# Delta rule, routed experts and a second FFN on one core: key products made further ahead, fewer conversions beside the last expert, token rows of block 1 fetched later

## The chip, the cores and the metric

One core of a Trainium2 chip runs one program that holds all three parts. The metric is the device time of one execution in microseconds (us). Three runs of the kernel before took 973.56, 974.29 and 976.66 us; the median, 974.29, is the time that the change is compared with.

## The reference

The first part is a delta rule over 768 tokens for 4 x 8 heads of size 48; the second sends each of 3072 tokens to one of 8 experts; the third is an FFN with squared ReLU.

```python
for t in range(S):                       # 768 tokens, state 48 x 48 per head
    y[:, :, t] = einsum('bhd,bhde->bhe', q[t], state)
    v_old = einsum('bhde,bhd->bhe', state, kt)          # kt: normalized key
    state += bt * einsum('bhd,bhe->bhde', kt, vt - v_old)
x = y.reshape(3072, 384)
expert_idx = argmax(xn @ en.T / tau)                    # one expert per token
out[mask] = gate_w * (relu(x[mask] @ w1[e]) @ w2[e])    # 8 experts, 384-1024-384
h = relu(out @ w_in)                                    # 384-2048
result = (h * h) @ w_out                                # 2048-384
```

## The kernel before

**Delta rule (0 to about 271 us).** The 768 tokens are 24 chunks of 32, and each chunk is a step `s` of one loop (`attention`). A step is a chain: the state `Sb` gives `ch` (L313), VectorE (DVE) writes half of `Ub` (L324) and ScalarE (ACT) the other half (L334), TensorE (PE) multiplies by the chunk's inverse table (L343), DVE and ACT copy that to `Wb` (L324, L356), PE adds to the state (dS, L362), ACT copies the state out (L372). A step is marked in the trace by DVE's `Ub` at L324; step 0 starts at 49.28 us.

The inverse tables are made by DVE for four chunks at once, a *stream* (`lanes`, L236 on): 31 rounds of a product (`mul`, L269, into `tmp`) and a sum (`acc`, L277, into `TL`). `acc` of a round reads what its `mul` wrote, and the next `mul` reads what `acc` wrote. `fill(now, part)` issues such operations at fixed places of a step, so many as the pace of the open streams asks for; with two streams open it takes from them by turns.

A stream needs the products of keys with keys of its four chunks. `gram(s)` (L154) makes them for one chunk, on PE, between W (L343) and the state's update (L362); ACT empties the two banks into `GPs` and `Pm` (L174). After every fourth chunk SP, the queue that issues most transfers, writes them to DRAM and reads them back in another layout (L176, L179, L184, L188). `gram(s)` needs the chunk's keys and queries, which `load_kq` fetches, three chunks to a buffer `W`, also on SP. SP, PE, DVE and ACT each work through their own instructions strictly in program order.

**Experts (about 272 to 556 us).** For expert e PE makes the hidden rows block by block (`fb` 0 to 7); ACT and DVE split each into two parts (`hh`, `hl`, L1173, L1174). `ht` (L1184) is their sum for the last 64 slots, which PE reads at L1208. Between these, the 64-bit numbers of `w_in` and `w_out` are turned into 32-bit ones on DVE and ACT, in 28 pieces of six operations each (`w64`, L1070 to L1090), and written to DRAM by a POOL queue transfer (L1083); `run(due, now, nq)` issues `nq` of these operations. Their buffers `t2k` are two, and `ht` and the one-hot tables of the last tokens (`ohs`, L1245) take turns in the same two. `place` (L926) multiplies by those tables; its result are rows of the second FFN's first block.

**Second FFN (about 556 us to the end).** 8 blocks of 384 tokens. `load_x2(n)` (L1135) fetches block n's token rows from DRAM, where the scatters of the experts (L1216) wrote them; `weights` fetches the converted pieces (L602) and splits them (L576, L579) during block 0.

Of the kernel before, what the change touches and what calls it, by code (L numbers as in the profile page):

```python
# [8 lines left out]
F32 = mybir.dt.float32  # L9
# [12 lines left out]
def kernel(  # L22
# [102 lines left out]

    def load_kq(s):
        if s % 3 == 0:
            KQ3[0] = cp.tile([128, 3, 4, 4, 2, C], F32, name="W", bufs=5)
        a = KQ3[0][:, s % 3]
        KQ[s] = a[:, :, :, 0], a[:, :, :, 1], a  # L130
        nc.sync.dma_start(a, kq[s])
# [14 lines left out]
    def gram(s, n0=0, n1=2, banks=GP2):  # L146

        g, i = divmod(s, 4)
        n = n1 - n0
        for p in range(4):  # L150
            for h2 in range(2):
                for b in range(4):
                    r = 64 * h2
                    PE.matmul(  # L154
                        banks[h2][C * b : C * b + C, p * n * C : (p + 1) * n * C],
                        KQ[s][0][r : r + 64, p, b],
                        KQ[s][n0][r : r + 64, p, b]
                        if n == 1
                        else KQ[s][2][r : r + 64, p, b].rearrange("d n j -> d (n j)"),
                        start=True,  # L160
                        stop=True,
                    )
        if i == 0 and n0 == 0:
            GPs[g] = gp.tile([128, 4, 8, C], F32, name="GPs", bufs=3)
        if i == 0 and n1 == 2:
            Pm[g] = gp.tile([128, 4, 4, 2, C], F32, name="Pm", bufs=3)
        for m in range(n0, n1):
            for h2 in range(2):
                if m == 0:
                    o = GPs[g][:, i].rearrange("p (x a c) j -> p c x a j", x=2, c=2)[:, h2]  # L170
                else:
                    o = Pm[g][:, :, i].rearrange("p (a c) x j -> p c x a j", c=2)[:, h2]
                src = banks[h2][:, : 128 * n].rearrange("p (x a n j) -> p n x a j", x=2, a=2, n=n)
                A.activation(o, src[:, m - n0], AF.Copy)  # L174
        if i == 3 and n0 == 0 and g > 1:
            nc.sync.dma_start(gscr[g % 2].rearrange("b i u j -> (b i) (u j)"), GPs[g].rearrange("p s h j -> p (s h j)"))  # L176
            ALs[g] = wp.tile([128, C, C], F32, name="AL", bufs=3)
            for b in range(4):
                nc.sync.dma_start(ALs[g][C * b : C * b + C], gscr[g % 2][b].rearrange("i u j -> u i j"))  # L179
        if i == 3 and n1 == 2:  # L180
            scr = pscr[g % 2]
            PL2[g] = gp.tile([128, 4, 4, 2, C], F32, name="PL2", bufs=4)
            for b in range(4):
                nc.sync.dma_start(  # L184
                    scr[:, :, b, :].rearrange("f j x -> j f x"),
                    Pm[g][C * b : C * b + C].rearrange("p f s c j -> p f (s c j)"),
                )
            nc.sync.dma_start(  # L188
                PL2[g].rearrange("p b s c j -> p (b s c j)"), scr.rearrange("f j b x -> (f j) (b x)")
            )  # L190
# [450 lines left out]
    def attention():  # L641
# [129 lines left out]
        for s in range(NS):  # L771
            g, i = divmod(s, 4)
            last = g == NG - 1
            while s not in ready:
                streams[0].pop()
            if s:
                mmV(s, 0)
                mmV(s, 1)
                mm1K(s, 0)
                mm1K(s, 1)  # L780
            U(s)
            fill(s, 0.25)
            if s:
                mm1Q(s)
            if s > 0:
                xT = xrt(s - 1)
            while streams and streams[0].g <= g:
                streams[0].pop()
            W(s, 0)
            W(s, 1)  # L790
            if s == NS - 1:
                lows.pop(0)()
            if s == 0:
                for b in range(4):
                    masked(0, b)
            if ahead < min(15 if s < 4 else NS, s + 12):
                gram(ahead)
                ahead += 1
            if scats and s >= E:
                drain(route_q)  # L800
                scats.pop(0)()
            fill(s + 0.25, 0.4)
            if s == NS - 4:
                first_x()
            if s >= NS - 3:
                pre1(s - NS + 3, False)
            if scats and s >= NS - 10:
                scats.pop(0)()
            if R is not None and s in (6, 10, 14, 17, 19):
                drain(route_q)  # L810
                R[1]()
                queue(R[2])
                scats += R[3]
            if s > 0:
                xlog(s - 1, xT)
                if i == 0 or s == 18:
                    R = route(g, 0, 2) if i else route(g - 1, 2 if s == 20 else 0, 4)
                    R[0][0]()
                    queue(R[0][1:])
                    if last and i == 0:  # L820
                        drain(route_q)
            if s + 1 < NS:
                dS(s, 0)
                dS(s, 1)
            if s == NS - 1:
                R = route(NG - 1, 2, 3)
                for o in R[0]:
                    o()
            PW(s)
            if last and i == 0:  # L830
                R[1]()
                queue(R[2])
                scats += R[3]
            if s <= E:
                padding(s)
            if i == 3 and g + 2 < NG:
                load_v(g + 2)
                load_k2(g + 2)
            if s % 3 == 2:
                for n in range(s + 13, min(s + 16, NS)):  # L840
                    load_kq(n)
            if ahead % 4 == 0 and ahead // 4 - 1 > made:
                made += 1
                streams.append(Stream(made, s + 1.6))
            fill(s + 0.65, 0.35)
            if s in (15, 17, 20):
                pre1((15, 17, 20).index(s), True)
            if s in (NS - 3, NS - 2):
                R = route(g, s - NS + 3, s - NS + 4)
                for o in R[0] + [R[1]] + R[2]:  # L850
                    o()
                scats += R[3]
# [241 lines left out]
    def moe():  # L1094
# [48 lines left out]
        for e in range(E):  # L1143
# [21 lines left out]
            for fb in range(8):  # L1165
# [11 lines left out]
                if fb == 3 and e + 1 < E:  # L1177
                    load_x(e + 1)
                if e:
                    run(fb + 1, 4, 2 if e + 1 == E else (1, 1, 0, 1, 0, 1, 0, 1)[fb])  # L1180
                else:
                    run(fb + 1, (0, 0, 0, 0, 2, 4, 6, 9)[fb], 1)
            ht = mp.tile([128, 8, 64], F32, name="t2k", bufs=2)
# [66 lines left out]
        for o in late:  # L1250
            o()
        for n in range(NBLK):
            if n + 1 < NBLK:
                load_x2(n + 1)
            xhn, xln = xh[f"a{n}"], xl[f"a{n}"]
            sh, sl = [
# [4 lines left out]
            for fb in range(16):  # L1261
# [13 lines left out]
                def part2(fb=fb, s2=s2, sh=sh, sl=sl):  # L1275
                    A.activation(sh[fb], s2, AF.Copy)
                    V.tensor_tensor(sl[fb], s2, sh[fb].bitcast(F32), ALU.subtract)

                if n == 0:
                    weights(10 * E + 2 + (fb + 1) * 8 // 15)  # L1280
            part2()
# [76 lines left out]
```

## Time and profile before

| | us |
|---|---|
| median of three runs | 974.29 |
| profiled execution | 973.39 |
| its span, first to last instruction | 971.6 |
| PE busy | 908.7 (94%) |
| DVE busy | 620.7 (64%) |
| ACT busy | 443.6 (46%) |
| steps 4 to 15 of the delta rule | 119.75, of which DVE is busy 107.85 |

The profiled execution is 0.9 us below the median, and 1.8 us of it lie around the span. The busy shares are means over three stages. From about 271 us on PE is busy nearly without a gap; in the delta rule its busy time contains stretches at a lower clock and small products that wait for nothing but the chain.

### The profile page before, as it was taken

The numbers are of one execution on the slowest core, as the hardware profiler recorded it, in microseconds if no ns is written. First come the engines' busy times: TensorE is split into PE (matmuls) and PEld (weight loads), VectorE is DVE, ScalarE is ACT, GpSimd is POOL, SyncE is SP. The second block draws the span as 40 slices with busy tenths as digits, with TensorE's granted clock in tenths as the row PEclk, the third lists the DMA queues.
The fourth block names the chain that finished last, engine by engine and source line by source line (L and its number), as shares of the span: only waits on it lengthen the run. The fifth ranks groups of instructions, "written<-read, shape, count | busy, mean of one in ns | idle before, by whom it ended". The sixth has DMA issues, their size and how long they took to land. (4 is left out here: it accounts for less than half of the span.)

```text
span 971.6 us, 22202 instructions
## 1 busy us (share of the span) xinstructions
PE 908.7 (94%) x8982; PEld 810.4 (83%) x8982; DVE 620.7 (64%) x1641; ACT 443.6 (46%) x1051; POOL 89.4 (9%) x126
## 2 busy tenths in 40 slices
PE   4778889899999999999999899999999999999998
PEld 3456667677777798888887689999999999999998
DVE  7999997899667888888789572423334241516060
ACT  2247656557734555455555362423333242415150
POOL 2000012011211122212211200000000000000000
PEclk7579988789989999999999999999999999999999
DMA  8667865441145677477557450101010101010000
GB/s 322 204 186 230 251 172 191 102 144 58 65 142 187 214 245 243 133 245 252 175 181 241 147 163 17 33 9 42 9 41 9 41 9 41 1 49 1 25 1 25
DMA packets 70608, 117.75 MB, mean 121 GB/s; under 512 B 22659, under 2 KB 48746, under 8 KB 70496
## 3 DMA queue, kind: packets, MB, share of 16 engines
q1 hardware_dynamic: 60784, 94.08, 30.4%
q0 software_dynamic: 5440, 15.88, 4.3%
q10 hardware_dynamic: 4272, 6.28, 2.0%
q8 instruction: 72, 1.18, 0.5%
q14 instruction: 40, 0.33, 0.1%
HBM read 84.12 MB, written 32.89 MB: 120 GB/s over the span
## 5 line engine op out<-in xcount | busy, mean ns | idle before, releaser
L1272 DVE TENSOR_TENSOR t4k<-t2k 128x384 f32<-128x384 f32 x128 | 71.4, 558 | 231.9 <-ACT t2k L1271 231.3
L277 DVE TENSOR_TENSOR TL<-TL,tmp 128x31 f32<-128x31 f32 (+15 forms) x186 | 62.7, 340 | 3.6
L269 DVE TENSOR_TENSOR tmp<-AL,TL 128x31 f32<-128x31 f32 (+15 forms) x186 | 62.4, 339 | 3.3
L1121 PE MATMUL gp<-wb,hh 128*128 128x384 f32 x184 | 62.9, 342 | 0.0
L1123 PE MATMUL gp<-wb,hl 128*128 128x384 f32 x184 | 62.0, 337 | 0.6 <-DVE hl L1174 0.6
L1122 PE MATMUL gp<-wb,hh 128*128 128x384 f32 x184 | 61.8, 336 | 0.0
L372 ACT ACTIVATE Sb<-sp 48x384 f32<-48x384 f32 x92 | 44.6, 484 | 34.0 <-PE sp L362 32.5
L1121 PE MATMUL sp<-xh,W 128*128 128x384 f32 (+1 forms) x150 | 51.0, 340 | 2.2 <-ACT t2k L1271 2.2
L1122 PE MATMUL yp<-xl,W 128*128 128x384 f32 (+1 forms) x153 | 52.6, 344 | 0.1
L1121 PE MATMUL yp<-xh,W 128*128 128x384 f32 (+1 forms) x153 | 52.5, 343 | 0.2 <-ACT xh L950 0.2
L1123 PE MATMUL yp<-xh,W 128*128 128x384 f32 (+1 forms) x153 | 52.6, 344 | 0.0
L1123 PE MATMUL gp<-xh,W 128*128 128x384 f32 (+1 forms) x153 | 52.1, 340 | 0.0
L1121 PE MATMUL gp<-xh,W 128*128 128x384 f32 (+1 forms) x153 | 52.0, 340 | 0.0
L1122 PE MATMUL gp<-xl,W 128*128 128x384 f32 (+1 forms) x153 | 51.9, 340 | 0.0
L362 PE MATMUL sp<-Wb,kL 128*48 128x96 f32 x736 | 49.5, 291 | 2.3 <-issue 1.4
L1121 PE MATMUL xp<-wb,hh 128*128 128x384 f32 x152 | 51.3, 338 | 0.0
L1123 PE MATMUL sp<-xh,W 128*128 128x384 f32 (+1 forms) x150 | 51.2, 341 | 0.0
L1123 PE MATMUL xp<-wb,hl 128*128 128x384 f32 x152 | 51.1, 336 | 0.0
L1122 PE MATMUL xp<-wb,hh 128*128 128x384 f32 x152 | 51.1, 336 | 0.0
L1122 PE MATMUL sp<-xl,W 128*128 128x384 f32 (+1 forms) x150 | 50.9, 340 | 0.0
L1216 POOL DMA_INDIRECT x<-y,rows x32 | 35.4, 1105 | 127.2 <-ACT y L1213 72.6
L362 PEld LDWEIGHTS sp<-Wb,kL 128*48 128x48 f32 x736 | 41.7, 149 | 6.0 <-ACT Wb L356 2.6
(314 smaller groups left out, 2463.7 us busy)
## 6 DMA issues: line engine op xcount, KB each, us to landing
W<-in_moe_w_dram SPq DMA_DIRECT2D x42, 256.0 KB, 3.6
W<-in_kq_dram SPq DMA_DIRECT2D x20, 512.0 KB, 7.0
hb<-in_moe_w_dram SPq DMA_DIRECT2D x24, 384.0 KB, 3.3
t4k<-in_moe_w_in_dram SPq DMA_DIRECT2D x12, 512.0 KB, 4.2
t4k<-in_moe_w_out_dram SPq DMA_DIRECT2D x16, 384.0 KB, 3.7
W<-wscr SPq DMA_DIRECT2D x16, 384.0 KB, 4.1
xs<-padrow ACTq DMA_DIRECT2D x8, 693.0 KB, 5.1
xe<-xs SPq DMA_DIRECT2D x8, 594.0 KB, 8.3
```

The source lines that it names most:

```text
L269: V.tensor_tensor(tv[0], AL[:, j, j + 1 :].unsqueeze(1).broadcast_to([128, n, m]), T[:, :n, j : j + 1].broadcast_to([128, n, m]), ALU.mult,)
L277: V.tensor_tensor(T[:, : j + 1, j + 1 :], T[:, : j + 1, j + 1 :], tv[0], ALU.add)
L362: PE.matmul(SP_[hq][64 * par : 64 * par + D, b * 96 : b * 96 + 96], kL2[g][:, i, b * 2 + hq], Wb[hq].rearrange("p b (m r) e -> p b r m e", ...
L372: A.activation(Sb[hq][r : r + D, :, :, par, :], SP_[hq][r : r + D, 0:384].rearrange("p (b m e) -> p b m e", b=4, m=2), AF.Copy,)
L1121: PE.matmul(ps, hs, rh, start=first, stop=False)
L1122: PE.matmul(ps, hs, rl, start=False, stop=False)
L1123: PE.matmul(ps, ls, rh, start=False, stop=last)
L1216: to_x2 = lambda n=n, t=t, y=y, rows_e=rows_e: G.indirect_dma_start(out=x2, out_offset=bass.IndirectOffsetOnAxis(ap=rows_e[:n, t : t + 1]. ...
L1272: V.tensor_tensor(s2, r, r, ALU.mult)
```

## The change

- Delta rule: `gram` may run up to 15 chunks ahead and not 12, and from step 2 on a step may make two chunks' products, until the lead is reached. With that the loads of keys and queries move: chunks 15 to 17 are fetched in step 0 into a buffer of their own, and the later ones three steps earlier. A stream is opened as soon as its four chunks' products are issued. `GPs` and `Pm` have two buffers and not three.
- Last expert: the conversions beside its hidden blocks are 2, 2, 2, 2, 2, 2, 0, 0 operations per block and not 2 in each; the rest stands later.
- Second FFN: the rows of block 1 are asked for in block 0 at `fb` 9, and no longer before block 0.

```diff
     def load_kq(s):
         if s % 3 == 0:
-            KQ3[0] = cp.tile([128, 3, 4, 4, 2, C], F32, name="W", bufs=5)
+            KQ3[0] = (wp if s == 15 else cp).tile([128, 3, 4, 4, 2, C], F32, name="W", bufs=1 if s == 15 else 5)
...
-            GPs[g] = gp.tile([128, 4, 8, C], F32, name="GPs", bufs=3)
+            GPs[g] = gp.tile([128, 4, 8, C], F32, name="GPs", bufs=2)
...
-            Pm[g] = gp.tile([128, 4, 4, 2, C], F32, name="Pm", bufs=3)
+            Pm[g] = gp.tile([128, 4, 4, 2, C], F32, name="Pm", bufs=2)
...
-            if ahead < min(15 if s < 4 else NS, s + 12):
-                gram(ahead)
-                ahead += 1
+            for _ in range(2 if s > 1 else 1):
+                if ahead < min(15 if s < 3 else 18 if s < 4 else NS, s + 15):
+                    gram(ahead)
+                    ahead += 1
...
+            if s == 0:
+                for n in range(15, 18):
+                    load_kq(n)
...
             if s % 3 == 2:
-                for n in range(s + 13, min(s + 16, NS)):
+                for n in range(s + 16, min(s + 19, NS)):
                     load_kq(n)
-            if ahead % 4 == 0 and ahead // 4 - 1 > made:
+            while ahead // 4 - 1 > made:
                 made += 1
                 streams.append(Stream(made, s + 1.6))
...
-                    run(fb + 1, 4, 2 if e + 1 == E else (1, 1, 0, 1, 0, 1, 0, 1)[fb])
+                    run(fb + 1, 4, ((1, 1, 0, 1, 0, 1, 0, 1), (2, 2, 2, 2, 2, 2, 0, 0))[e + 1 == E][fb])
...
         for n in range(NBLK):
-            if n + 1 < NBLK:
+            if 0 < n < NBLK - 1:
                 load_x2(n + 1)
...
+                if n == 0 and fb == 9:
+                    load_x2(1)
```

By this, `gram` runs for chunk 12 in step 0, 13 in step 1, 14 in step 2, 15 and 16 in step 3, 17 and 18 in step 4, and 19 to 23 in steps 5 to 9; before it ran for chunk s + 11 in each of the steps 1 to 12. The streams of chunks 12 to 15, 16 to 19 and 20 to 23 open in steps 3, 5 and 9, and before in 4, 8 and 12.

**DVE in step 7**, right behind `Wb`. Names are the buffers: `AL` the products, `TL` the table, `tmp1` the product of a round; `sm` a small table of a newly opened stream. Before:

```order
L269 TENSOR_TENSOR tmp1_2246<-AL_1714,TL_1949 128x156
L277 TENSOR_TENSOR TL_1949<-TL_1949,tmp1_2246 128x6x26
L269 TENSOR_TENSOR tmp1_2249<-AL_1714,TL_1949 128x175
L277 TENSOR_TENSOR TL_1949<-TL_1949,tmp1_2249 128x7x25
L269 TENSOR_TENSOR tmp1_2252<-AL_1714,TL_1949 128x192
L277 TENSOR_TENSOR TL_1949<-TL_1949,tmp1_2252 128x8x24
L269 TENSOR_TENSOR tmp1_2255<-AL_1714,TL_1949 128x207
L277 TENSOR_TENSOR TL_1949<-TL_1949,tmp1_2255 128x9x23
```

Now:

```order
L269 TENSOR_TENSOR tmp1_2373<-AL_1594,TL_1895 128x156
L277 TENSOR_TENSOR TL_1895<-TL_1895,tmp1_2373 128x6x26
L249 COPY sm_2080<-AL_2018 128x32
L269 TENSOR_TENSOR tmp1_2379<-AL_1594,TL_1895 128x175
L77 TENSOR_SCALAR sm_2080<-sm_2080 128x32
L277 TENSOR_TENSOR TL_1895<-TL_1895,tmp1_2379 128x7x25
L79 TENSOR_TENSOR sm_2080<-magic_69,sm_2080 128x32
L269 TENSOR_TENSOR tmp1_2384<-AL_1594,TL_1895 128x192
L82 TENSOR_TENSOR sm_2080<-sm_2080 128x32
L277 TENSOR_TENSOR TL_1895<-TL_1895,tmp1_2384 128x8x24
```

Where one stream alone filled the step, each row reading what the row above it wrote, the rows of two streams now alternate.

**SP from the end of step 3's exchange on** (difference; `-` before, `+` now): `PL_841`, `PL_1719` and `PL_1599` are products read back, `W` keys and queries, `vV` and `kL` values and keys of four chunks.

```order
 L188 DMA PL_841<-pscr_64 128x1024
-L131 DMA W<-in_kq_dram 128x1024 x3
-L140 DMA vV<-in_v_dram 128x1536
-L144 DMA kL_1602<-in_k_dram 128x1536
+L131 DMA W<-in_kq_dram 128x1024 x6
 L176 DMA gscr_67<-GPs 128x1024
 L179 DMA AL<-gscr_67 32x32x32 x4
 L184 DMA pscr_65<-Pm 32x4x256 x4
```

Six loads of keys and queries (chunks 15 to 20) now stand in front of the next exchange, and the values and keys of chunks 8 to 11 (`vV`, `kL`) behind it; chunks 21 to 23 stand behind the exchange after that one.

**DVE at the end of the last expert**, from the last but one `hl` on: `hl` and `ht` (here `t2k_7918`, now `t2k_7910`), conversions of pieces (`t2k_7857`, `t2k_7913`), `W_4590` a split of weights, the small `gate` and `gsm` rows of the routing weight. Before:

```order
L1174 SCALAR_TENSOR_TENSOR hl_7758<-gp0_106,hh_7757 128x448
L1090 TENSOR_TENSOR t2k_7857<-t2k_7857,W_4822 128x384
L1082 SCALAR_TENSOR_TENSOR t2k_7857<-t4k_7791,t2k_7857 128x384
L1174 SCALAR_TENSOR_TENSOR hl_7758<-sp1_104,hh_7757 128x448
L579 TENSOR_TENSOR W_4590<-W_4822,W_4307 128x768
L910 TENSOR_REDUCE gsm_7752<-glg_7754 128x4
L1070 TENSOR_SCALAR W_4822<-t4k_7855 128x384
L911 TENSOR_SCALAR gsm_7752<-gsm_7752 128x4
L1074 SCALAR_TENSOR_TENSOR t2k_7913<-t4k_7855,W_4822 128x384
L912 RECIPROCAL gate_7755<-gsm_7752 128x4
L1184 TENSOR_TENSOR t2k_7918<-hh_7757,hl_7758 128x512
```

Now (the lines of this part are 4 higher):

```order
L1178 SCALAR_TENSOR_TENSOR hl_7758<-gp0_106,hh_7757 128x448
L1178 SCALAR_TENSOR_TENSOR hl_7758<-sp1_104,hh_7757 128x448
L579 TENSOR_TENSOR W_4590<-W_4822,W_4307 128x768
L914 TENSOR_REDUCE gsm_7752<-glg_7754 128x4
L915 TENSOR_SCALAR gsm_7752<-gsm_7752 128x4
L916 RECIPROCAL gate_7755<-gsm_7752 128x4
L1188 TENSOR_TENSOR t2k_7910<-hh_7757,hl_7758 128x512
L579 TENSOR_TENSOR W_4590<-W_4822,W_4307 128x768
L1094 TENSOR_TENSOR t2k_7857<-t2k_7857,W_4822 128x384
L1086 SCALAR_TENSOR_TENSOR t2k_7857<-t4k_7791,t2k_7857 128x384
L1074 TENSOR_SCALAR W_4822<-t4k_7855 128x384
L1078 SCALAR_TENSOR_TENSOR t2k_7949<-t4k_7855,W_4822 128x384
```

`ht` moves ahead of the end of piece `t2k_7857` and of the start of the next piece. The buffers alternate, so `ht` takes the buffer of the piece before `t2k_7857`, and the next piece (`t2k_7949`) that of `t2k_7857` itself, two rows of DVE after its end.

## Rows read from the trace of the kernel before

**Rows 1.** Windows, steps 7, 9, 12, sum of 4-15: length, busy by engine, PEclk.

```profile
117.71:129.33 11.62, 9.30 (x216) 6.95 (x212) 9.72 (x28) 6.15 (x18) 0.00 (x0) 0.85 0.45 157
...
139.40:150.12 10.72, 9.32 (x170) 7.19 (x174) 8.34 (x28) 4.50 (x13) 2.94 (x3) 0.68 0.81 170
...
171.35:183.45 12.10, 10.80 (x170) 8.07 (x174) 9.49 (x29) 4.50 (x13) 1.15 (x1) 0.58 0.43 101
...
sum 119.75, PE 104.38 PEld 79.79 DVE 107.85 ACT 71.79 POOL 13.78; mean PE 8.70 PEld 6.65 DVE 8.99 ACT 5.98 POOL 1.15
```

**Rows 2.** Waits of DVE in steps 4 to 15: total, times, longest.

```profile
DVE Ub L324 <- PE ch L313: 7.8, 4, 2.3
```

**Rows 3.** Waits of PE in the same stretch.

```profile
PE ch L343 <- DVE Ub L324: 10.3, 7, 2.4
PE xp L425 <- issue: 2.3, 1, 2.3
```

**Rows 4.** Timeline of DVE, one stream alone: start, duration, line, operation, wait before.

```profile
126.88 0.41 DVE L277 TENSOR_TENSOR TL<-TL,tmp 128x240 f32<-128x240 f32 x1
127.32 0.41 DVE L269 TENSOR_TENSOR tmp<-AL,TL 128x247 f32<-128x247 f32 x1
...
129.33 0.96 DVE L324 TENSOR_TENSOR Ub<-ch,blk 128x768 f32<-128x768 f32 x1 [1.15 <-PE ch L313]
```

**Rows 5.** Timeline of DVE, a row that something else follows.

```profile
163.64 0.27 DVE L277 TENSOR_TENSOR TL<-TL,tmp 128x112 f32<-128x112 f32 x1
163.84 0.95 DVE L324 TENSOR_TENSOR Wb<-ch,blk 128x768 f32<-128x768 f32 x1
```

**Rows 6.** Timeline of SP, steps 8 and 9: start, duration, transfer.

```profile
133.19 0.33 SPq L176 DMA_DIRECT2D gscr<-GPs  x1
...
146.75 0.34 SPq L188 DMA_DIRECT2D PL<-pscr  x1
147.19 1.32 SPq L131 DMA_DIRECT2D W<-in_kq_dram  x3
```

**Rows 7.** Page, transfers: KB each, median us from issue to landing.

```profile
W<-in_kq_dram SPq DMA_DIRECT2D x20, 512.0 KB, 7.0
```

**Rows 8.** Timeline of PE and ACT in step 5: key products and emptying.

```profile
102.49 0.86 PE L154 MATMUL gp<-W 64*32 64x64 f32 x64
...
103.69 0.45 ACT L174 ACTIVATE GPs<-gp 128x128 f32<-128x128 f32 x2
```

**Rows 9.** Waits of PE from 530 to 575 us.

```profile
PE xp L1208 <- DVE t2k L1184: 3.8, 1, 3.8
PE sp L1121 <- ACT t2k L1271: 2.2, 1, 2.2
PE ch L926 <- DVE t4k L1230: 0.9, 1, 0.9
```

**Rows 10.** Timeline of POOL and DVE, end of the last expert.

```profile
533.24 0.54 POOL L1083 DMA_DIRECT2D wscr<-t2k  x1 [6.34 <-DVE t2k L1082]
537.05 0.69 DVE L1184 TENSOR_TENSOR t2k<-hh,hl 128x512 f32<-128x512 f32 x1 [1.66 <-DMA wscr<-t2k]
547.24 0.56 POOL L1083 DMA_DIRECT2D wscr<-t2k  x1 [2.46 <-DVE t2k L1082]
551.31 0.42 DVE L1245 TENSOR_SCALAR t2k<-t4k,xe 128x384 fp32r<-128x384 int32 x1 [2.58 <-DMA wscr<-t2k]
```

**Rows 11.** Windows behind PE's waits at L1208 and in block 0.

```profile
537.90:541.30 3.40, 3.40 (x12) 1.35 (x14) 2.92 (x6) 0.00 (x0) 0.28 (x1) 0.50 0.57 173
568.60:572.00 3.40, 3.40 (x12) 3.40 (x11) 3.27 (x6) 2.89 (x7) 0.00 (x0) 0.50 0.48 133
```

**Rows 12.** Timeline of SP and ACT, start of the second FFN.

```profile
560.69 0.37 SPq L1135 DMA_DIRECT2D xe<-x  x1
561.15 1.39 SPq L602 DMA_DIRECT2D W<-wscr  x3
565.75 0.84 ACT L576 ACTIVATE wb<-W 128x768 fp32r<-128x768 f32 x1 [4.38 <-DMA W<-wscr]
```

## The prediction

> **What bounds the kernel now.** I read the page's busy shares first, then the windows of single steps, then who waits for whom, and last the timelines around the places that the change touches. In the delta rule, steps 4 to 15 take 119.75 us; DVE is busy for 107.85 of them and PE for 104.38 [rows 1]. DVE waits there for PE only four times, 7.8 us in all, always for the product that `Ub` is made of [rows 2]; PE waits for DVE seven times, 10.3 us, at the start of W [rows 3]. So in most of these steps DVE, not PE, sets the length, and its work is 119.75 - 7.8 = 111.95 us: 107.85 of busy time and 4.1 us of small gaps. The four waits of DVE end the steps 7, 9, 10 and 12; of the three that are shown, two have a granted clock of 0.68 and 0.58 [rows 1]: with 1.0 and 0.5 as its two levels (2.4 and 1.2 GHz) 64% and 84% of these steps ran at the lower one, and there the chain over PE sets the length. From 272 us on PE is the bound, with two holes: 3.8 us at L1208 in the last expert, where PE waits for `ht`, and 2.2 us in the second FFN's block 0 [rows 9].
>
> **DVE's order in the delta rule.** The number of DVE operations stays the same; only what stands behind what changes. Within one stream each row reads what the row above wrote: L277 at 126.88 takes 0.41 us and the next starts at 127.32, 0.03 after its end [rows 4]. Where the next row is of other data it starts before the end: L277 at 163.64 takes 0.27, and `Wb` starts at 163.84, 0.07 before it is over [rows 5]. The difference is 0.10 us by these rounded rows; over all such pairs of the steps 0 to 22 (176 of the first kind, of which rows 4 show one, and 118 of the second) it is 0.116. In program order I counted the rows of L269 and L277 whose next DVE row uses their result: 176 before and 74 now, 102 fewer. That is 10.2 to 11.8 us of DVE time, taken as 11.0, all of it in steps 4 to 15, where two streams are now open together; the steps 0 to 3 and 16 to 23 hold the same DVE work as before. The largest piece is step 7: 22 such pairs before, one now, and some larger operations moved out, 3.1 us in all. Steps 9, 10 and 12 together have 1.4 us less.
>
> The Trainium skill speaks against this term. "VectorE: DVE Perf Modes", section "The DRAIN you can't avoid", says that the pipeline empties behind every DVE operation before the next starts, and that chaining without semaphores does not avoid it; its rules for authors ask for fewer operations only. By that the term would be 0. The trace does not agree, since the row behind 163.64 starts 0.07 us before its end [rows 5]; the page itself adds that a next operation that isn't held starts earlier. I keep it as a rival.
>
> **What of it reaches the end.** Of the 11.0 us, 1.4 lie in steps 9, 10 and 12, which end with DVE waiting: they give nothing at first. Step 7's 3.1 us meet a new wait. `gram(21)` now runs in step 7, on PE, ahead of the routing product and of the state's update, and its keys are fetched on SP behind the exchange of products that step 5 starts. In the trace that exchange goes from 133.19, 3.9 us after its step's start, to 146.75, and the keys behind it go out at 147.19, 14.0 us after its first transfer [rows 6]. So they go out some 17.9 us after step 5 begins, and 7.0 us is the median to land [rows 7], which contains the crowded loads of the opening. `gram(21)` is reached some 19 us after the start of step 5 (two steps of 8 to 9 us and 2.2 into the third). Its wait is between 0 (if the load lands in 1 us) and 6 us (7.0); I take 4, since the three loads share their 7.0. Step 7 of before had 2.3 us of PE standing still in the same place [rows 3], so that step stays at about 11.6 us, and the 3.1 are lost. There remain 11.0 - 1.4 - 3.1 = 6.5 us.
>
> Steps 3 and 4 make two chunks' products each. One costs PE 0.86 us, and the second of a pair finds its two banks full until ACT, busy with `Wb` until then, has emptied them: four rows, two of them 0.45 us as a pair, from 103.69 on [rows 8]. The second pair moves the state's update some 2.1 us later in each of the two steps. DVE's own rows cover a part, since no wait of DVE ends the steps 4 to 6 before [rows 2]: the cost is 0 (covered) to 4.2 (nothing covered), taken as 1.5, nearer to the covered end for that reason. Fewer buffers for `GPs` and `Pm` and the loads of values behind the exchange have nothing that waits for them in time by the same rows; up to 1 us stays in the range for them.
>
> Last the clock. 7.8 us of DVE waits [rows 2] are left, in steps where PE ran at its lower level; before those stretches PE had been waiting for DVE (10.3 us in all, [rows 3]). With 11 us less of DVE work these waits of PE shrink. What comes back lies between 0 and 7.8 us; nothing in the trace decides it, and I take a third, 2.6. The delta rule comes to -6.5 + 1.5 - 2.6 = **-7.6 us**, with ends at -12.8 (all 7.8 back) and +1.5 (nothing saved, rival C).
>
> **The last expert.** `ht` waited 1.66 us for the landing of a store that POOL issued at 533.24, 3.8 us before, and PE waited 3.8 us for `ht` [rows 9, 10]; 3.4 us at half clock followed [rows 11]. Now `ht` takes a buffer whose store is long done and stands before four conversion rows: PE's wait falls to about 0.5, a gain of 3.3. But the next piece takes the buffer of the one finished right behind `ht`. Its store goes out at about 537.3 and lands 3.8 later, at 541.1; DVE stands until then, ACT's copy of the t = 3 rows behind it, and two pieces have still to be done. The last store goes out at 548.2 to 549.6 instead of 547.24. The second one-hot table waits for its landing, 4.07 us after issue before (547.24 to 551.31, [rows 10]), and PE's `place` for the table. So `place` comes 1.0 to 2.4 us later, and the 3.3 us that PE gained are spent in waiting there: about 0.9 + 3.3 + 1.7 = 5.9 us in one hole, longer than the 3.8 that a half-clock stretch followed (3.4 us at half speed give 1.7 us less work). Bounds: -1 (the store lands in time and `place` is early) to +4.1; I take **+2.5**.
>
> **Block 1's rows.** SP issued the fetch of block 1's rows at 560.69, and only behind it, at 561.15, the converted weights; ACT waited 4.38 us for these, until 565.75 [rows 12], PE 2.2 us [rows 9], and a half-clock stretch of 3.4 us followed, 1.7 us lost [rows 11]. The fetch stood in the queue for the last scatter of the experts, and the weights had been converted long before. Now the weights go out as soon as a buffer is free, the stall is gone, and nothing else is due before: -2.2 to -3.9, taken as **-3.5**. The rows themselves are asked for at `fb` 9, 9 us ahead of their use.
>
> **Sum.** 973.39 - 7.6 + 2.5 - 3.5 = 964.8 for a profiled execution; the median stands 0.9 above it: 965.7, **966 us**.
>
> **Rivals.**
> B, the clock stays up: the four waits of DVE vanish. For it: they stand only in steps with half-clock stretches or the standstill of step 7. Against: a step's products on PE stay small and wait for the chain. 973.39 - 12.8 + 2.5 - 3.5 + 0.9 = 960.5.
> C, the saved DVE time turns into waiting: `Ub` waits for PE's product in every step. For it: PE's busy time is 104.38 of 119.75 [rows 1], so 8.7 of 10 us a step, and the chain over ACT's copies is as long. Or the alternation saves nothing; that is the skill's rule. Then only the costs of the delta rule are left, +1.5: 973.39 + 1.5 + 2.5 - 3.5 + 0.9 = 974.8.
> D, slower: the keys of chunk 21 come late. The place is PE in step 7. If they take the full 7.0 us, PE stands for 6, which is 3.7 more than step 7's standstill of before, and two half-clock stretches of 1.7 us follow in steps 7 and 8; every later step hangs on it, and the saved DVE time is spent waiting. 974.8 + 3.7 + 3.4 = 981.9. It decides from a landing of some 5 us on, if at the same time the DVE saving is idle. Against: the loads before landed in time for their products.
>
> **Chances.** A, the forecast, 0.50, with 962 to 970 as its own range; B 0.18; C 0.20; D 0.12. About 0.3%, 2.9 us, is what a measurement of this kernel can tell from no change: faster lies below 971.4 and slower above 977.2. Faster takes 0.46 of A, all of B and 0.04 of C: 0.68. Slower takes D but 0.01 and 0.03 of C: 0.14. 0.18 stays for the same. The range goes from B (half of B, 0.09, below 960) to just above C, 976; above lies D with a few hundredths of C.
>
> **What would show it.** In the trace of the changed kernel: the steps 4 to 15 at about 111 us, with DVE busy some 7 us less (102 times the 0.07 of rows 5, since rows that overlap count once) and its small gaps some 3 us less (102 times the 0.03 of rows 4); L269 and L277 followed within their own end by another stream's row; a PE wait of about 4 us in front of the products of step 7; PE's wait at L1212 (before L1208) under 1 us, but a wait of DVE at the piece behind `ht` of 3 to 4 us and a PE wait at `place` of 5 to 6; no wait of PE in block 0. Wrong would be: DVE waiting for PE in most steps (C), no alternation gain at all, or a standstill of 6 us and more in step 7 (D).

## The result: 1.0% faster, and where the time came from

Over all runs on the same chips the changed kernel takes 962.76 us (median; 958.08 to 969.78) and the kernel before 973.02. The ratio is 0.9904, with a 95% interval from 0.9879 to 0.9929. The forecast was 966 us, or 0.9915 of 974.29. One execution of the kernel with the rows edit undone (below) took 2149.24 us, is counted as slow and stands in that kernel's median (962.94; 961.45 without it) but not in its ratio.

The profiled execution of the changed kernel takes 958.54 us and is one of its quick ones; the one of before, 973.39, lies near its median. So the two profiles differ by 15 us where the medians differ by 10 (9.3 by the ratio). By stages (starts of the steps from the timeline of DVE, the rest from that of PE):

| us | before | changed |
|---|---|---|
| until step 0 | 49.28 | 50.39 |
| steps 0 to 3 | 41.42 | 41.62 |
| steps 4 to 15 | 119.75 | 108.29 |
| of these, steps 9 to 15 | 71.05 | 57.85 |
| steps 16 to 23 and what follows, to the first expert | 69.04 | 67.70 |
| experts | 276.84 | 277.32 |
| second FFN | 415.27 | 411.19 |

The windows of the changed kernel's steps 5, 6, 7, 9 and 12 and the sum of steps 4 to 15 (columns as in [rows 1]):

```profile
101.70:113.03 11.33, 8.82 (x240) 6.51 (x232) 7.87 (x33) 7.94 (x23) 0.00 (x0) 1.00 0.96 302
113.03:124.76 11.73, 10.72 (x184) 8.15 (x188) 8.74 (x37) 4.51 (x13) 0.00 (x0) 0.56 0.72 170
124.76:133.54 8.78, 7.53 (x217) 5.75 (x209) 7.96 (x29) 6.17 (x18) 0.95 (x1) 1.00 0.75 236
...
142.44:149.99 7.55, 7.55 (x217) 5.96 (x209) 7.55 (x28) 6.20 (x18) 4.21 (x4) 1.00 0.40 149
...
167.04:175.97 8.93, 8.39 (x188) 6.26 (x176) 8.89 (x36) 6.74 (x18) 3.64 (x5) 1.00 0.26 98
...
sum 108.29, PE 97.58 PEld 74.76 DVE 99.87 ACT 71.50 POOL 16.47; mean PE 8.13 PEld 6.23 DVE 8.32 ACT 5.96 POOL 1.37
```

DVE is busy for 99.87 us instead of 107.85, 8.0 less with the same operations. Without its waits (below) its small gaps are 108.29 - 99.87 - 7.3 = 1.1 us instead of 4.1, 3.0 less. Steps 9 and 12, which ran mostly at half clock before, now run at full clock in 7.55 and 8.93 us. Steps 5 and 6 have got longer by 6 us together: they hold a new wait. The waits of DVE and of PE in these twelve steps:

```profile
DVE Ub L324 <- PE ch L313: 3.8, 3, 2.9
DVE vV L259 <- DMA vV<-in_v_dram: 3.5, 1, 3.5
```

```profile
PE ch L343 <- DVE Ub L324: 6.6, 4, 3.2
PE gp L154 <- DMA W<-in_kq_dram: 1.2, 1, 1.2
```

Against [rows 2, 3], 7.8 has become 3.8 and 10.3 has become 6.6, but DVE now waits 3.5 us for values (`vV`), and PE 1.2 for keys. In steps 9 to 15 alone DVE's waits for PE's product are nearly gone; before and now:

```profile
DVE Ub L324 <- PE ch L313: 6.6, 3, 2.3
```

```profile
DVE Ub L324 <- PE ch L313: 0.2, 1, 0.2
```

So 3.6 of the 3.8 us lie in steps 4 to 8, where it was 1.2 before. How DVE's rows follow each other in step 7 is seen in its timeline, at the place that answers to [rows 4]:

```profile
127.98 0.31 DVE L269 TENSOR_TENSOR tmp<-AL,TL 128x156 f32<-128x156 f32 x1
128.32 0.32 DVE L277 TENSOR_TENSOR TL<-TL,tmp 128x156 f32<-128x156 f32 x1
128.56 0.18 DVE L249 COPY sm<-AL 128x32 f32<-128x32 f32 x1
128.68 0.34 DVE L269 TENSOR_TENSOR tmp<-AL,TL 128x175 f32<-128x175 f32 x1
128.94 0.17 DVE L77 TENSOR_SCALAR sm<-sm 128x32 int32<-128x32 int32 x1
```

L277 reads what L269 wrote and starts 0.03 us behind its end; the copy of the other stream starts 0.08 before L277 has ended, and so does the row behind 128.68.

The end of the last expert: POOL's stores, DVE's next piece and the second table (start, duration, wait before), answering to [rows 10].

```profile
526.00 0.57 POOL L1087 DMA_DIRECT2D wscr<-t2k  x1 [1.79 <-DVE W L1074]
...
534.26 0.57 POOL L1087 DMA_DIRECT2D wscr<-t2k  x1 [2.56 <-DVE t2k L1086]
```

```profile
522.17 0.66 DVE L1188 TENSOR_TENSOR t2k<-hh,hl 128x512 f32<-128x512 f32 x1
...
526.07 0.56 DVE L1078 SCALAR_TENSOR_TENSOR t2k<-t4k,W 128x384 int32<-128x384 int32 x1
...
537.88 0.46 DVE L1249 TENSOR_SCALAR t2k<-t4k,xe 128x384 fp32r<-128x384 int32 x1 [2.13 <-DMA wscr<-t2k]
```

The piece behind `ht` starts at 526.07, 0.07 us after POOL began to issue the store of the piece in front: it waits for no store. PE's waits from 515 to 560 us, against [rows 9], and the clock behind the last one, against [rows 11]:

```profile
PE ch L930 <- DVE t4k L1234: 2.2, 1, 2.2
PE ch L930 <- ACT y L1217: 1.7, 1, 1.7
PE xp L1212 <- DVE t2k L1188: 1.3, 1, 1.3
```

```profile
537.10:543.90 6.80, 5.04 (x22) 5.04 (x23) 3.12 (x5) 1.26 (x2) 2.43 (x2) 0.50 0.44 128
```

What PE no longer waits at L1212 it waits at `place` (L930), 3.9 us, and in this profile 6.8 us at half clock go with that. In block 0 no wait is left.

### The profile page after: what moved, and what is told of

Its sections match the earlier page's. It is cut to its first block, busy times and chain, and to the rows that moved or that the text cites. A ratio compares the mean times of both kernels' runs of the same rounds, so it can differ in the third digit from the quotient of the medians.

```text
span 956.5 us, 22209 instructions
## 1 busy us (share of the span) xinstructions
PE 897.4 (94%) x8982; PEld 803.9 (84%) x8982; DVE 612.9 (64%) x1641; ACT 444.3 (46%) x1051; POOL 90.6 (9%) x126
## 3 DMA queue, kind: packets, MB, share of 16 engines
q10 hardware_dynamic: 4272, 6.28, 2.0%
## 5 line engine op out<-in xcount | busy, mean ns | idle before, releaser
L277 DVE TENSOR_TENSOR TL<-TL,tmp 128x135 f32<-128x135 f32 (+15 forms) x186 | 60.8, 337 | 1.8
L269 DVE TENSOR_TENSOR tmp<-AL,TL 128x135 f32<-128x135 f32 (+15 forms) x186 | 60.7, 337 | 1.6
L1299 ACT ACTIVATE y<-xp 128x384 f32<-128x384 f32 x12 | 5.9, 492 | 89.2 <-PE xp L1127 89.2
L1299 ACT ACTIVATE y<-gp 128x384 f32<-128x384 f32 x12 | 5.9, 492 | 88.3 <-PE gp L1127 88.3
```

Source lines behind the costliest of these rows:

```text
L269: V.tensor_tensor(tv[0], AL[:, j, j + 1 :].unsqueeze(1).broadcast_to([128, n, m]), T[:, :n, j : j + 1].broadcast_to([128, n, m]), ALU.mult,)
L277: V.tensor_tensor(T[:, : j + 1, j + 1 :], T[:, : j + 1, j + 1 :], tv[0], ALU.add)
L1299: A.activation(y, ps[:, :DM], AF.Copy)
```

## The experiments

Theory A: DVE sets the length of the steps, and what the change gives is the order of its rows: fewer of them wait for the row above. Its rivals here: B, that products and loads come earlier, or that the other two edits made the gain (the prediction's own rival B, on the clock, is taken up further below); C of the prediction, that the order of DVE's rows costs nothing. Each kernel ran 6 or 12 times. Times are medians; ratios are to the kernel before on the same chip, with their intervals. For "3 to 8" and "9 to 15" read the sum of these steps in the profiled execution (before: 57.76 and 71.05; changed: 59.52 and 57.85).

**The delta rule alone.** The kernel before with only the edits of the change's first bullet, two of which are these (cut):

```diff
-            if ahead < min(15 if s < 4 else NS, s + 12):
+                if ahead < min(15 if s < 3 else 18 if s < 4 else NS, s + 15):
...
-            if ahead % 4 == 0 and ahead // 4 - 1 > made:
+            while ahead // 4 - 1 > made:
```

> The kernel before with the change of the delta rule alone. By theory A (DVE's work falls by 102 rows that no longer wait for the row above, 0.10 to 0.116 us each, and DVE sets the length of the steps) it holds nearly all of the gain: 7 to 11 us faster than before, steps 4 to 15 near 108 us, the expert stage and the second FFN as before. By theory B (the gain is that of block 1's rows and of the expert stage, the delta rule only happened to have few half-clock stretches in the one profiled execution) it is within 3 us of before.

965.56 us, 0.9921 [0.9887, 0.9955]; 3 to 8 62.49, 9 to 15 57.93. That is 7.7 us of the change's 9.3, and the second FFN takes 415.29 us as before; steps 4 to 15 take 111.34 us where about 108 was expected. A holds against B's second half.

**The pauses alone.**

```diff
-                    run(fb + 1, 4, 2 if e + 1 == E else (1, 1, 0, 1, 0, 1, 0, 1)[fb])
+                    run(fb + 1, 4, ((1, 1, 0, 1, 0, 1, 0, 1), (2, 2, 2, 2, 2, 2, 0, 0))[e + 1 == E][fb])
```

> The kernel before with the conversion pauses of the last expert alone. The prediction's step said +2.5 us (bounds -1 to +4.1). By the trace of the changed kernel the piece behind ht takes ht's own buffer and not that of the piece before, so that DVE doesn't stand there: +0.5 us, between -1 and +1.5, with PE's wait at L1208 near 1.3 and a wait of 3 to 4 us at place, which a half-clock stretch follows. The stall of block 1 (2.2 us at L1121) stays.

971.90 us, 0.9981 [0.9958, 1.0003]. Experts 277.29 us, +0.45; PE waits 1.3 us at L1208 and 3.7 at `place`. The 0.45 is not a cost that is shown: with the same code of this stage the experts took 274.33 to 277.70 us in seven profiles (of the changed kernel, of this one, and of five below that touch neither the pauses nor the table), and without the pauses 276.49 to 277.64 in three. Within the seven, the time goes with the half clock behind the wait at `place`: none in the profile with 274.33, 3.4 us in those with 275.14 and 275.21, 6.8 us in the four from 277.12 on. The second FFN takes 411.34, and PE has no wait in block 0: the expectation that this stall stays was wrong.

**Block 1's rows alone.**

```diff
-            if n + 1 < NBLK:
+            if 0 < n < NBLK - 1:
                 load_x2(n + 1)
...
+                if n == 0 and fb == 9:
+                    load_x2(1)
```

> The kernel before with the later fetch of block 1's rows alone. Expected: the 2.2 us wait of PE in block 0 and the half-clock stretch of 3.4 us behind it are gone, 3.5 to 4 us faster, and the other stages as before. If the clock falls there anyway (its stretch belongs to something else than this wait): 2.2 us.

970.91 us, 0.9984 [0.9960, 1.0009]. Experts 276.49, second FFN 411.37, no wait in block 0. The stages give 3.9 us; the median gives 1.6, with an interval that just reaches 3.9.

**The order of DVE's rows.** In the changed kernel, product and sum of a round as one piece for the streams from chunk 12 on:

```diff
-            for f in (mul, acc):
-                add(lambda f=f, j=j: f(j), (31 - j) * (j + 1))
+            if g > 2:
+                add(lambda j=j: (mul(j), acc(j)), c=0.2 + (31 - j) * (j + 1) / 480)
+            for f in (mul, acc) if g < 3 else ():
+                add(lambda f=f, j=j: f(j), (31 - j) * (j + 1))
```

> The changed kernel, but the product and the sum of a round are issued as one piece in the streams of the chunks 12 to 23, so that each sum stands right behind the product that it reads: 77 rows more than in the changed kernel whose next DVE row uses their result, with the same operations, the same key products and the same loads. By theory A DVE's work rises by 77 x 0.10 to 0.116 = 7.7 to 8.9 us in steps 6 to 18, and the delta rule gets 4 to 8 us longer (some of it lies in the steps that wait for a load). By rival C of the prediction and the page's rule that every DVE operation empties the pipeline, the order costs nothing: within 1.5 us of the changed kernel.

975.03 us, 1.0016 [0.9988, 1.0043]: the whole gain is gone, 12.3 us between the medians where 4 to 8 were expected. Not all of it is DVE's order, since PE waits 8.7 us for the keys of chunk 21 in this profile (3 to 8 71.32). Steps 9 to 15, behind that, take 65.75 instead of 57.85 us: 7.9 us for 49 more such rows, of which DVE's waits for PE and ACT are 1.5 (0.2 in the changed kernel). DVE is busy for 61.28 us there instead of 57.21. C is out.

**The streams opened late**, with everything else as early as in the changed kernel:

```diff
-            while ahead // 4 - 1 > made:
+            while ahead // 4 - 1 > made and s >= 4 * made - 4:
```

> The changed kernel with the key products and all loads as early as there, but the streams of the chunks 12 to 23 opened in steps 4, 8 and 12 as before: DVE's rows follow each other as in the kernel before (102 more that use the result of the row above). By theory A (order of DVE's rows) the delta rule loses 8 to 11 us against the changed kernel, steps 4 to 15 come near 119 us, and the whole stands 3 to 4 us below the kernel before, which are the experts and the second FFN: about 969. By theory B (early products and loads are what counts) it stays within 2 us of the changed kernel.

974.58 us, 1.0021 [0.9996, 1.0046]; 9 to 15 67.49, +9.6 for 64 more such rows. This is slower than the 969 that was expected, and its profile (968.18) is the quickest of its executions. The early products and loads alone give nothing in sum: by this profile they gain 3.6 us in steps 9 to 15 (71.05 before) and lose 5.2 in steps 3 to 8 (62.94; 57.76 before). B is out as the source of the gain. The window of steps 9 to 15, of the changed kernel and of this one:

```profile
142.44:200.30 57.86, 54.05 (x1118) 41.65 (x1106) 57.21 (x198) 39.78 (x105) 15.52 (x15) 0.94 0.41 126
```

```profile
144.35:211.84 67.49, 56.88 (x1079) 43.00 (x1079) 62.12 (x210) 39.27 (x103) 11.31 (x13) 0.90 0.36 113
```

DVE is busy 4.9 us longer. Some 0.6 of it, an estimate from the means of the changed kernel's rows, are other operations: the streams that open late leave 12 more in these steps, 210 against 198, and on the whole smaller ones. Over steps 4 to 15, which hold the same operations, it is 108.29 against 99.87, 8.4 us or 0.08 for each of the 102 rows, which is the overlap. In steps 9 to 15 DVE stands still for 5.4 us instead of 0.7. The rows' own gaps, 64 x 0.03, are 1.9 of these 4.7; the other 2.8 are waits (0.2 in the changed kernel):

```profile
DVE Ub L324 <- PE ch L313: 2.0, 1, 2.0
DVE Wb L324 <- ACT Wb L356: 1.0, 1, 1.0
```

**Values ahead.**

```diff
+            if i == 3 and g + 2 < NG:
+                load_v(g + 2)
             for _ in range(2 if s > 1 else 1):
...
             if i == 3 and g + 2 < NG:
-                load_v(g + 2)
                 load_k2(g + 2)
```

> The changed kernel with the load of the values of four chunks issued ahead of the step's key products, so that on SP it stands before their exchange and not behind it. In the changed kernel DVE waits 3.46 us in step 5 for the values of the chunks 8 to 11, and 10.2 us at half clock follow from 113.8 us on. Expected: this wait is gone, step 5 falls from 11.3 to about 8 us and the stretch with it; but gram(21) comes sooner and waits longer for its keys than the 1.25 us of there, 4 to 6 us, so that the delta rule gains 0 to 5 us. If the half clock has nothing to do with the wait, and the wait only moves: 0.

966.00 us, 0.9919 [0.9893, 0.9944]. DVE's wait for the values is gone (steps 5 and 6: 7.78 and 8.66 us), and PE waits 6.28 us for keys in step 7 (16.96); step 3 takes 12.18 instead of 9.08 (11.93 in two other profiles that have the changed kernel's delta rule). The wait moved; nothing was gained.

**Values and keys ahead.**

```diff
+            if i == 3 and g + 2 < NG:
+                load_v(g + 2)
+            if s % 3 == 2:
+                for n in range(s + 16, min(s + 19, NS)):
+                    load_kq(n)
             for _ in range(2 if s > 1 else 1):
                 if ahead < min(15 if s < 3 else 18 if s < 4 else NS, s + 15):
                     gram(ahead)
...
-                load_v(g + 2)
                 load_k2(g + 2)
-            if s % 3 == 2:
-                for n in range(s + 16, min(s + 19, NS)):
-                    load_kq(n)
```

> As the one with the values ahead, and the keys and queries of the chunks 18 to 23 are issued ahead of the step's key products too, so that those of 21 to 23 stand before the exchange of the chunks 16 to 19. Expected: neither the wait for values nor that for keys is left, steps 5 to 7 take about 8.0, 9.0 and 7.6 us (31.8 in the changed kernel), and the delta rule is 5 to 7 us shorter than there: about 956 to 958. If the exchange, now behind 1.5 MB of keys, comes too late for the stream of the chunks 16 to 19, DVE stands still in step 7 or 8 for 3 to 5 us instead and half of that is lost again.

962.83 us, 0.9881 [0.9831, 0.9930]. Neither wait is left (1.1 us for the products of the chunks 16 to 19 are new in step 7), but steps 3 and 6 take 14.12 and 12.02 us, with PE standing there for nothing that the profile shows (1.7 and 2.8 us) and partly at half clock (a mean of 0.76 and 0.86): the 5 to 7 us did not come.

**The same, and the second one-hot table in a buffer that no store uses.**

```diff
-                    ohs = [None] + [mp.tile([128, BW], F32R, name="t2k", bufs=2) for _ in range(2)]
+                    ohs = [None] + [mp.tile([128, BW], F32R, name=o, bufs=b) for o, b in (("t2k", 2), ("junk", 1))]
```

> As the one with both loads ahead, and the second one-hot table of the last expert gets a buffer that no conversion uses, so that it doesn't wait for the last store (2.13 us in the changed kernel, with PE waiting 2.19 for it and a half-clock stretch of 6.8 us behind). Expected: PE's place starts 2 us earlier, the expert stage falls by 2 us, by up to 5 where the clock stays up. If the rows of y hold it (PE waits 1.7 us for ACT there too): below 1 us.

956.75 us, 0.9821 [0.9779, 0.9863]: the lowest ratio of all, and faster than the changed kernel by their intervals. The experts take 274.27 us. That the table gave 3 us of it isn't shown, since the stage took as little as 274.33 us with the table where it was.

**The table alone**: the last diff on the changed kernel.

> The changed kernel with the second one-hot table in a buffer of its own, and the loads as in the changed kernel. It tells what of the time of the kernel with both loads ahead and the table apart is the table's. Expected: PE's wait of 2.19 us for that table at place is gone, the expert stage takes 274 to 275 us and not 277.3, and the whole is 2 to 4 us faster than the changed kernel: near 959 to 961. If it were the loads that made the other one faster: 0 to 1 us.

960.45 us, 0.9888 [0.9853, 0.9923]; experts 272.68. The wait for the table is gone from PE's list; only 1.8 us for ACT's `y` stay at `place`. In this profile PE waits 10.1 us for keys in step 7. By the ratio that is 1.6 us faster than the changed kernel, with intervals that overlap: neither the loads nor the table alone is clear of it, and how the gain of both divides between them stays open. In the four profiles with this table the experts took 272.68 to 274.29 us, just below the 274.33 to 277.70 of the seven with the pauses and the table in its old place.

**The rows edit undone** in the changed kernel: the diff of block 1's rows, backwards.

> The changed kernel with the rows of block 1 asked for before block 0, as before the change. In the kernel with the pauses alone PE had no wait in block 0 any more and the second FFN took 411.3 us, as with the later rows. So by theory A (the pauses alone take that stall away, since the scatter that the rows wait for comes sooner) it is within 1 us of the changed kernel. By the prediction's step (the later rows take it away) the stall of 2.2 us and a half-clock stretch come back: 3.5 us slower.

962.94 us, 0.9903 [0.9868, 0.9938], and a second FFN of 411.34 us: the same as the changed kernel. Its delta rule is word for word the changed kernel's, but its profile shows another execution of it. PE's waits in steps 4 to 15 and SP's from 95 to 132 us:

```profile
PE gp L154 <- DMA W<-in_kq_dram: 10.3, 1, 10.3
```

```profile
SPq L144 <- DMA xs<-padrow: 8.5, 1, 8.5
SPq L179 <- DMA gscr<-GPs: 7.2, 1, 7.2
```

SP stands 8.5 us at a load of keys (`kL`, L144) until a store of padding rows has landed that ACT's queue issued; all that is queued behind it, the exchange and the keys of chunk 21, comes later. In the changed kernel's profile this wait is 4.9 us. The wait is the program's own: in the program that the changed kernel is built into, the transfers of SP's and ACT's queues take eight landing semaphores in turn, the load uses the one that a padding store used last, and an instruction in front of it waits until that count is complete.

**One key ahead.** On the kernel with both loads ahead and the table apart:

```diff
-            if s % 3 == 2:
-                for n in range(s + 16, min(s + 19, NS)):
-                    load_kq(n)
+            if s % 3 == 2 and s + 16 < NS:
+                load_kq(s + 16)
             for _ in range(2 if s > 1 else 1):
...
+            if s % 3 == 2:
+                for n in range(s + 17, min(s + 19, NS)):
+                    load_kq(n)
```

> As the one with both loads ahead and the table apart, but only the first of the three chunks of keys ahead of the exchange, the other two behind it. There the exchange stood behind 1.5 MB of keys and DVE waited 1.1 to 2.6 us in step 7 for the products of the chunks 16 to 19. Expected: that wait falls under 1 us and gram(21) finds its keys, steps 5 to 8 take 33 to 35 us in sum (39.9 there), so that the whole is 2 to 4 us below it. If gram(22) and gram(23) then wait for theirs: as there.

956.72 us, 0.9847 [0.9812, 0.9881]; steps 5 to 8 take 40.9 us. `gram(22)` waits 3.4 us for its keys, and DVE's wait for the products of the chunks 16 to 19 is still 1.9: as the last sentence of its expectation had it, nothing gained.

**The padding stores moved** out of steps 3 to 5, on top of the kernel with both loads ahead and the table apart.

```diff
-            if s <= E:
-                padding(s)
+            for n in {0: (0,), 1: (1,), 2: (2,), 6: (3, 4, 5), 7: (6, 7), 8: (8,)}.get(s, ()):
+                padding(n)
```

> As the one with both loads ahead and the table apart, but the stores of padding rows (693 KB each, from ACT's queue, one in each of the steps 0 to 8) leave the steps 3 to 5: three go out in step 6 and two in step 7. In the other kernels SP stands at a load in step 4 or 5 until such a store has landed: 4.9 us in the changed kernel, 8.5 in the one with the rows edit undone, 6.8 and 5.6 in the one with both loads ahead. Expected, if these stores are what makes keys and exchange late: SP's waits for them are gone between 95 and 125 us, the keys of chunk 21 go out near 104 and not at 110.4, DVE has no wait for the products of the chunks 16 to 19 in step 7, steps 3 to 8 fall from 61.6 us to 54 to 58, and the whole is 3 to 6 us faster than that kernel. If the crowd of transfers itself is what makes them late: within 2 us of it, and the waits stand at other transfers.

957.84 us, 0.9837 [0.9802, 0.9872]; 3 to 8 62.00 against 61.57. SP no longer waits for padding, the keys of chunk 21 go out at 104.76, DVE has no wait for the products in step 7: that part is shown. The time stays. The five stores were only moved: they go out between 119.36 and 128.72, beside the steps 7 and 8, so that whether they or the other transfers make these steps long isn't separated. The steps 7 and 8 of this kernel:

```profile
121.44:131.45 10.01, 7.15 (x181) 5.10 (x177) 7.94 (x29) 6.15 (x18) 0.95 (x1) 1.00 0.91 270
131.45:144.55 13.10, 10.86 (x217) 8.30 (x210) 8.96 (x35) 6.15 (x18) 2.29 (x4) 0.74 0.84 279
```

The transfers are 0.91 and 0.84 busy there, and PE's standstill is again one for which the profile names nothing (its waits from 60 to 145 us):

```profile
PE gp L154 <- issue: 3.2, 2, 2.2
PE ch L313 <- issue: 2.1, 2, 1.5
```

## Why the prediction was right, and which of its steps were not

- **The order of DVE's rows: right in mechanism, and the main term.** 102 rows at 0.10 to 0.116 us were forecast as 11.0 us of DVE time. In steps 4 to 15 DVE's busy time fell by 8.0 us and its gaps by 3.0, 11.0 together ("some 7 us" and "some 3 us" had been named as its signs). In steps 9 to 15, which no load disturbs, 64 such rows fewer are 7.0 us by that price. These steps fell by 13.2 from before to the changed kernel, and by 9.6 against the kernel with late streams, which runs with the old order. The two kernels with the old order or a part of it lose 7.9 and 9.6 us there. By the rule of the Trainium skill ("VectorE: DVE Perf Modes", section "The DRAIN you can't avoid") the order would cost nothing; these runs speak against that reading, and the rows at 128.32 and 128.56 show the next operation starting 0.08 us before the end.
- **The clock: too small.** A third of the 7.8 us of DVE's waits was taken to come back, 2.6. In steps 9 to 15 it was nearly all, 6.6 down to 0.2, which is the rest of the 13.2 (13.2 - 7.0 = 6.2), and steps 9 and 12 run at full clock. The prediction's rival B was right for these steps. With the streams opened late 3.0 of the 6.6 are left: so 3.6 came back with the earlier key products, four chunks of which PE made in steps 9 to 12 before and one now, and 2.8 with DVE's shorter rows. The prediction put all of it down to the latter. Whether the clock or PE's smaller work ended the waits isn't separated.
- **The loads: wrong in place, and in size.** The prediction had a wait of 4 us for the keys of chunk 21 in step 7 (0 to 6) and up to 1 us for the values. In the changed kernel's profile DVE waits 3.46 us for the values in step 5, a stretch of 10.2 us at half clock follows (step 6 has a mean of 0.56), and the keys cost only 1.25 us since the two steps before had grown. In two other profiles of the same code the keys cost 10.1 and 10.3 us, outside the range; this is a sign that the prediction gave to rival D, but with DVE's saving kept the second of these executions, at 968.66 us, is still faster than the kernel before. The step that failed is "they go out some 17.9 us after step 5 begins": 3.9 us to the start of the exchange and 14.0 from there to the keys were carried over from before. In the new order the exchange has the loads of values and keys (`vV`, `kL`) in front of it (the list of SP's transfers in "The change" begins in step 1, where `PL_841` is read back at 64.84, and not in step 3), `kL` waits for a padding store, and the keys went out 20.5 and 26.3 us after the step began: the exchange started 5.3 and 6.9 us into the step, and it was 15.3 and 19.4 us from there. So the wait in front is the smaller part of the 8.4 us in the second case; there the landing of the exchange's own first store took 7.2 us of SP's time (3.2 at most before), and why is open. Step 7, forecast at 11.6 us, took 8.78, 7.98, 20.06 and 20.26 us in the four profiles of this delta rule. The steps 3 to 8 took 59.5, 62.5, 68.7 and 69.1 us in these four, and the steps 4 to 15 108.29, 111.34, 114.12 and 115.27, so that the table above shows the best case. It fits the wide spread of the changed kernel's times (958 to 970); that it is all of it isn't shown.
- **The double products: about right.** PE waits 1.0 to 1.1 us in front of the second product in steps 3 and 4; these steps took 9.08 and 9.69 us against 9.06 and 10.01, so that it was covered. In two of the four profiles it was not: step 3 ran partly at half clock there (a mean of 0.71) and took 11.93 us, still inside the 0 to 4.2 us that were given for both steps.
- **The last expert: +2.5 forecast, no cost shown (+0.5 between the two profiles).** PE's wait at L1208 fell as forecast (1.3; 0.5 had been said), and it came back at `place` as forecast (3.9; 5.9 had been said), with half clock behind. The step that failed is "the next piece takes the buffer of the one finished right behind `ht`". It takes `ht`'s own (in the built program both have the same address), whose reader on PE is done first in program order, and DVE doesn't stand; two buffers of one name need not take turns, as "The change" has it. The trace of before had shown this: there the second piece behind `ht` waits for PE's product at L1208, the reader of `ht`, and for no store. Its row in the timeline of DVE, kernel before:

```profile
542.33 0.56 DVE L1074 SCALAR_TENSOR_TENSOR t2k<-t4k,W 128x384 int32<-128x384 int32 x1 [1.34 <-PE xp L1208]
```

 So DVE lost nothing. What is left, 0.5 us, lies within the 274.33 to 277.70 us that this code takes from one profile to the next, with the half clock behind `place`.
- **Block 1's rows: the size right (4.1 us of the second FFN, 3.5 forecast), the cause only half.** Either edit takes the stall away alone, and the rows edit adds nothing to the pauses. The two terms were summed as if they stood apart; in truth the pauses, forecast as a cost, bring the 4 us that the rows edit was given.
- **The sum** came out because the gain by the clock and the losses by loads, both mis-sized, stand against each other: -7.6 forecast for the delta rule, 7.7 faster measured with it alone (interval 4.4 to 11.0). The term of DVE's order was foreseen; that the total came so near is luck.

## What to carry to other kernels

On an engine that sets the pace, count the rows that use the result of the row above: on this kernel each costs about 0.1 us, and two independent chains, taken by turns, take that away with no operation less. When work is made earlier, follow its loads along their queue and ask of every row in front of them what it may wait for, transfers of other queues among them. Before two edits are added up, ask whether they take away the same wait.

## What the runs showed of the hardware that was not expected

On DVE, a row whose operands the row above did not write started 0.08 us before that row's end, and one that reads its result 0.03 us behind it (128.32 and 128.56 above). A load on SP's queue waited for a store that ACT's queue had issued (8.5 us in one profile, 4.9 in another), though the two share no data; this is the program's sharing of semaphores, and with the padding stores moved the wait was gone. And PE stood 1 to 2.8 us at a time without a wait that the profile names: in the changed kernel 1.05 us in step 8, with the transfers 0.89 busy, and 2.2 and 1.5 us in the last experiment. Crowded transfers are not shown as its cause, since the kernel before has such a standstill of 2.3 us in step 7, with a share of 0.45 [rows 1, 3]. What PE waits for there was not settled. Nor was the clock: in the last expert a wait of 3.2 to 4.1 us at `place` was followed by none, 3.4 or 6.8 us at half clock, with the same code.
